# Weights that begin at four different byte offsets, by the step's number, in a one-core FFT and feed-forward kernel

## The chip, the cores and the metric

The kernel runs on one core of one Trainium2 chip. The metric is the device time of one execution in microseconds (us). TensorE (PE in the profile) multiplies, VectorE (DVE) and ScalarE (ACT) round, add and copy, GpSimd (POOL) folds inputs, SyncE (SP) issues most transfers. A matmul has two operands in the on-chip memory SBUF: the weights (stationary, 128x128), which a separate instruction LDWEIGHTS loads (PEld in the profile), and the moving operand, which is streamed past them. Its sum goes to PSUM.

## The reference

x is 8 x 3136 x 256. The real part of its two-dimensional Fourier transform over the last two axes is x'. Each row of x' (256 values) is normalized, goes through two matrices with a ReLU between them, and is added back:

```python
X = np.fft.fft(np.fft.fft(x, axis=1), axis=2)
x = X.real.astype(np.float32)
xn = (x - mean(x)) / sqrt(var(x) + 1e-06) * g_ln      # over the last axis
ch = np.maximum(xn @ w_ch1, 0.0) @ w_ch2              # 256 -> 1024 -> 256
return x + ch
```

## The kernel before

The first two thirds of the transform are small matmuls with tables of sines and cosines (lines 255 to 313: steps 1 and 2 of a mixed-radix transform, `step1`, `step2`). The last axis' transform is folded into the first matrix: `w1` is multiplied by a table in the prologue (`transform_w1`), so that the main loop multiplies the half-transformed rows (`ck`, "chunks" of 256 columns) straight by it. The residual x' itself comes from two short matmuls per tile with the table `ty_s` (`residual`, line 428).

The main loop runs over steps s. A chunk c has 8 steps, one for each 128 of the 1024 hidden values (f = s mod 8), and there are 49 chunks, so 392 steps. In a step

- `moe1_a(s)` multiplies the chunk by 128 columns of the first matrix: two halves j of three matmuls each (line 354), with weights `w1_hi` or `w1_lo` and moving operand `ckh` or `ckl` (`ck_hi`, `ck_lo`);
- ACT and DVE form h from the two halves (lines 359 to 361), `moe1_b(s - 1)` rounds the step before with ReLU into `h_hi` and what is left into `h_lo` (lines 368 and 369);
- `moe2(s - 3)` multiplies h of three steps back by the second matrix: four products of three matmuls each (line 404), with weights `h_hi` or `h_lo` and moving operand `w2_hi` or `w2_lo`.

Each product is three matmuls because the values are split into a rounded part (hi) and a rest (lo), both in the type fp32r; hi x hi, hi x lo and lo x hi are summed in PSUM. So a step has 6 + 12 = 18 matmuls of 256 columns, each with a weight load of its own. Between some steps stand the short matmuls of `step2` (line 309), `residual` (line 428), `step1` (line 262, three of 512 columns) and `step1_ends`.

The order on PE, ACT, DVE and POOL is the order in which the program is written (the tables `after` and `late` say behind which step a piece stands); a tile pool hands out buffers in turn by tag.

Two pools matter here. `moving` holds the moving operands, `weights` the weights. A tile `margin` makes the pool `moving` begin at a multiple of 256 bytes, and a tile `offset` of 64 bytes shifts everything in `weights`: `w1_hi`, `w1_lo`, the four buffers each of `h_hi` and `h_lo`, `t1_hi`, `t1_lo` and `s2` all begin 64 bytes past a multiple of 256. A slice of 128 columns is 512 bytes, so the weights of every matmul of lines 354 and 404 begin 64 bytes past a multiple of 256, and their moving operands at a multiple of 256.

`tw_all` (the table by which w1 is transformed) and `warm_h` (zeros for the matmuls that warm up TensorE) have memory of their own in the pool `const`.

Of the kernel before, what the change touches and what calls it, by code (L numbers as in the profile page):

```python
# [20 lines left out]
F32 = mybir.dt.float32  # L21
F32R = mybir.dt.float32r
# [6 lines left out]
NB, N, D, FF = 8, 3136, 256, 1024  # L29
# [7 lines left out]
MAXW = LASTR + 2 * NB  # L37
CKW = 320
HW = 576
NS = 14  # L40
ROWS = NB * N
NU = NS // 2
KP = 8 * NS

# [17 lines left out]
def tables():  # L62
# [15 lines left out]
    vs = ((0, np.arange(1, 15)), (1, np.append(np.arange(15, NV), 0)))  # L78
    tab = np.zeros((2, 2, 2, NS, 2, HALF))
    tz = np.zeros((4, NS, 50))  # L80
    t = 0
# [17 lines left out]
    tab = tab.transpose(3, 0, 1, 2, 4, 5).reshape(112, 2, HALF)  # L99
    tz = np.concatenate([tz.reshape(4 * NS, 50), np.zeros((KP - 4 * NS, 50))])  # L100
    d = np.arange(1, 129)[:, None]
# [17 lines left out]
def input_rows():  # L119
# [3 lines left out]

    v = np.full((2, NS), -1)
    v[0] = np.arange(1, 15)
# [21 lines left out]
def tile_kernel(ctx: ExitStack, tc: tile.TileContext, x, g_ln, w1, w2, tu, tab, tz, ty, tw, out):  # L147
    nc = tc.nc
    moving = ctx.enter_context(tc.tile_pool(name="moving", bufs=1))
    weights = ctx.enter_context(tc.tile_pool(name="weights", bufs=1))  # L150
    const = ctx.enter_context(tc.tile_pool(name="const", bufs=1))
    work = ctx.enter_context(tc.tile_pool(name="work", bufs=2))
# [3 lines left out]
    moving.tile([128, 32], F32, name="margin")  # L156
    w2_hi = moving.tile([128, 8, D], F32R, name="w2_hi")
    w2_lo = moving.tile([128, 8, D], F32R, name="w2_lo")
    weights.tile([128, 16], F32, name="offset")
    w1_hi = weights.tile([128, 2, FF], F32R, name="w1_hi")  # L160
    w1_lo = weights.tile([128, 2, FF], F32R, name="w1_lo")
    t1_hi = weights.tile([128, 128], F32R, name="t1_hi")
    t1_lo = weights.tile([128, 128], F32R, name="t1_lo")
    tu_s = const.tile([128, 388], F32, name="tu_s")
    tab_s = const.tile([KP, 2, HALF], F32, name="tab_s")
    tz_s = const.tile([KP, 50], F32, name="tz_s")
    tw_all = const.tile([128, 640], F32, name="tw_all")
    tw_s = tw_all[:, :512].rearrange("p (i j k) -> p i j k", i=2, j=2)
    minus = const.tile([128, 128], F32R, name="minus")
    ty_s = const.tile([128, 2, 130], F32, name="ty_s")  # L170
# [27 lines left out]
    def fold_zw(b, i, eng):  # L198

        if i > 3 and b == 0:  # L200
            t = weights.tile([128, HW], F32, tag="h_hi", name=f"zw{b}_{i}", bufs=4)
        else:
# [79 lines left out]
    def width(c):  # L282
        return MAXW if c == LC else CW

    def first_token(m):
        b, j = divmod(m, 8)
        return b * REG + max(gb[2 * j] - 2, 0)
# [52 lines left out]
    def moe1_a(s, passes=((0, 1), (1, 0), (0, 0))):  # L340
        c, f = divmod(s, 8)
        w = width(c)
        ch = chunk[c][1:]
        fs = slice(128 * f, 128 * f + 128)
        wt = (w1_hi, w1_lo)
        if w <= CW:
            ab = psum.tile([128, 2, CW], F32, tag="ab", name=f"ab{s}", bufs=2)
            pa, pb = ab[:, 0], ab[:, 1]
        else:
            pa = psum.tile([128, MAXW], F32, tag="ab", name=f"aa{s}", bufs=2)  # L350
            pb = psum.tile([128, MAXW], F32, tag="fft", name=f"bb{s}")
        for j, pt in ((0, pa), (1, pb)):
            for n, (wi, xi) in enumerate(passes):
                nc.tensor.matmul(pt, wt[wi][:, j, fs], ch[xi][:, j, :w],  # L354
                                 start=(n == 0), stop=(n == 2))
        asb = work.tile([128, MAXW], F32, tag="asb", name=f"asb{s}")
        h = hh[s] = work.tile([128, 2 * CW], F32, tag="h", name=f"h{s}", bufs=4)
        m = 2 * CW - w
        nc.scalar.copy(asb[:, :w], pa)  # L359
        nc.vector.tensor_tensor(out=h[:, :w], in0=asb[:, :w], in1=pb, op=ALU.add)  # L360
        nc.vector.tensor_tensor(out=h[:, w:], in0=asb[:, :m], in1=pb[:, :m], op=ALU.subtract)  # L361

    def moe1_b(s):
        h = hh[s]
        n = 2 * CW
        h_hi = weights.tile([128, HW], F32R, tag="h_hi", name=f"h_hi{s}", bufs=4)[:, :n]
        h_lo = weights.tile([128, n], F32R, tag="h_lo", name=f"h_lo{s}", bufs=4)
        nc.scalar.activation(h_hi, h, AF.Relu)  # L368
        nc.vector.scalar_tensor_tensor(out=h_lo, in0=h, scalar=0.0, in1=h_hi.bitcast(F32),  # L369
                                       op0=ALU.max, op1=ALU.subtract)  # L370
        hh[s] = (h_hi, h_lo)
# [195 lines left out]
    psw = {}  # L567
# [6 lines left out]
                             stop=(i == 1))  # L574

    def w1_cols(t, k, j):
        return t[:, j, 512 * k:512 * k + 512]

    def round_w1(k):
        for j in range(2):  # L580
            nc.scalar.copy(w1_cols(w1_hi, k, j), psw[k, j])

    def rest_w1(k):

        for j in range(2):
            nc.tensor.matmul(psw[k, j], minus, w1_cols(w1_hi, k, j), start=False, stop=True,
                             skip_group_check=True)

    def rest_w1_copy(k):
        for j in range(2):  # L590
            nc.scalar.copy(w1_cols(w1_lo, k, j), psw.pop((k, j)))

    def finish_w2(n):
        _, e, f = conv.pop(f"w2_{n}")
        nc.vector.scalar_tensor_tensor(out=f, in0=f, scalar=2.0 ** -20, in1=e, op0=ALU.mult,
                                       op1=ALU.mult)
        return f
# [19 lines left out]
    for m in range(3, 64):  # L617
        s = 8 * (first_token(m) // CW) - 3
# [26 lines left out]
    for c in range(LC):  # L645
        s = 8 * c + (5 if c > 1 else 6)
# [14 lines left out]
        add_late(8 * LC + y, residual_y, LC, i)  # L661

    warm = work.tile([128, 2 * D], F32, tag="fold", name="warm")
    warm_h = const.tile([128, 2 * D], mybir.dt.bfloat16, name="warm_h")

    def warm_up(n, zeros):

# [5 lines left out]
    with tc.manual_schedule(engines={E.PE, E.Activation, E.DVE, E.Pool}):  # L673
        with tc.manual_schedule(engines={E.SP}):
# [71 lines left out]
            transform_w1(0, 0)  # L746
            transform_w1(0, 1)
            round_w1(0)
            convert_m("w1_3", w1p[3])
            convert_b("w1_3")  # L750
# [8 lines left out]
            convert_z("w2_0", w2p[0])  # L759
            convert_z("w2_1", w2p[1])  # L760
            rest_w1_copy(0)
            transform_w1(1, 1)
            round_w1(1)
            convert_m("w2_0", w2p[0])
            convert_b("w2_0")
            f = finish_w2(0)
# [7 lines left out]
            step2(1, "hl", 0)  # L774
            f = finish_w2(1)
            moe1_a(0, ((1, 0), (0, 0), (0, 1)))
            split_w2(1, f)
            step2(0, "f")
            moe1_a(1, ((1, 0), (0, 0), (0, 1)))
            rest_w1(1)  # L780
            moe1_b(0)
            moe1_a(2)
            moe1_b(1)
            moe1_b(2)
            moe1_a(3)
            rest_w1_copy(1)
            step2(1, "f")
            convert_a("w2_2", w2p[2])
# [5 lines left out]
            f = finish_w2(2)  # L794
# [51 lines left out]
```

## Time and profile before

| what | before |
|---|---|
| device time, median of 3 runs | 1007.62 us (1007.08 to 1007.76) |
| the profiled execution | 1007.27 us, its span 1005.5 us |
| PE busy | 995.1 us, 99% of the span, 8289 matmuls |
| DVE, ACT, POOL busy | 812.3 us (81%), 540.1 us (54%), 243.9 us (24%) |
| granted TensorE clock | 1.000 |

The span runs from the first to the last instruction. A matmul's duration in the profile (276 to 286 ns for 256 columns) is longer than the distance from one start to the next, since matmuls overlap; where matmuls follow each other without a wait, it is the distance between starts that adds up to the span.

### The profile page before, as it was taken

What the parts mean: (1) busy time and instruction counts of PE and PEld (TensorE: products, weight loads), DVE (VectorE), ACT (ScalarE), POOL (GpSimd) and SP (SyncE); (2) the same over time, 40 slices, a digit from 0 to 9 for tenths busy, and PEclk for the clock granted to TensorE, in tenths of its full rate; (3) what the DMA queues carried; (4) which work ended last, traced back from release to release, by engine and by line L of the source; (5) the groups of instructions that cost most, each with busy time, mean ns of one, the idle gap of its engine ahead of it and who ended that gap; (6) DMA issues with size and microseconds to landing.
All of it is one profiled execution on the core that took longest, in us unless ns stands there. A gap on an engine that the chain in (4) does not pass through costs nothing.

```text
span 1005.5 us, 21770 instructions
## 1 busy us (share of the span) xinstructions
PE 995.1 (99%) x8289; PEld 973.7 (97%) x8289; DVE 812.3 (81%) x2190; ACT 540.1 (54%) x1416; POOL 243.9 (24%) x278
## 2 busy tenths in 40 slices
PE   9999999999999999999999999999999999999998
PEld 6799999999999999999999999999999999999998
DVE  7788887878787788878877887878788788887887
ACT  3655556554555555655456555555555554555553
POOL 2146414530153203440054401532034300000000
PEclk9999999999999999999999999999999999999999
DMA  9933243223122511333132232224101230100101
GB/s 346 266 141 126 85 143 110 86 84 108 62 95 85 157 44 53 103 120 105 44 111 101 74 106 75 84 96 126 55 32 44 74 105 23 43 22 22 43 22 43
DMA packets 41528, 92.10 MB, mean 92 GB/s; under 512 B 4176, under 2 KB 18704, under 8 KB 40528
## 3 DMA queue, kind: packets, MB, share of 16 engines
q1 hardware_dynamic: 40016, 88.87, 27.1%
q8 instruction: 66, 1.08, 0.5%
q0 software_dynamic: 320, 1.05, 0.3%
q10 hardware_dynamic: 1088, 0.79, 0.2%
q14 instruction: 38, 0.31, 0.1%
HBM read 50.32 MB, written 40.37 MB: 90 GB/s over the span
## 4 chain that ended last, share of the span: by engine, by line
PE 88%; DVE 7%; ACT 2%; DMA 2%; issue 1%; SPq 0%; ACTq 0%; DVEq 0%
PE acc L404 49%; PE ab L354 25%; PE ps L309 5%; PE psy L428 4%; PE ps L262 3%; DVE h_lo L369 2%; DVE h L360 1%; DVE h L361 1%; ACT h_hi L368 1%; PE ps L255 1%; PE ps L257 1%; DMA scratch<-s 1%; DMA s<-scratch 1%; DMA xs<-x 0%; DVE st L450 0%
## 5 line engine op out<-in xcount | busy, mean ns | idle before, releaser
L404 PE MATMUL acc<-w_hi,h_lo 128*128 128x256 f32 x1568 | 437.1, 279 | 0.2 <-DVE h_lo L369 0.2
L404 PE MATMUL acc<-w_hi,h_hi 128*128 128x256 f32 x1568 | 436.9, 279 | 0.0
L404 PE MATMUL acc<-w_lo,h_hi 128*128 128x256 f32 x1568 | 436.9, 279 | 0.0
L369 DVE SCALAR_TENSOR_TENSOR h_lo<-h,h_hi 128x512 fp32r<-128x512 f32 x392 | 285.9, 729 | 160.8 <-ACT h_hi L368 159.0
L368 ACT ACTIVATE h_hi<-h 128x512 fp32r<-128x512 f32 x392 | 250.1, 638 | 266.0 <-DVE h L361 265.5
L404 PEld LDWEIGHTS acc<-w_hi,h_hi 128*128 128x128 f32 x1568 | 296.7, 189 | 0.0
L404 PEld LDWEIGHTS acc<-w_lo,h_hi 128*128 128x128 f32 x1568 | 295.3, 188 | 0.0
L404 PEld LDWEIGHTS acc<-w_hi,h_lo 128*128 128x128 f32 x1568 | 294.6, 188 | 0.6 <-DVE h_lo L369 0.4
L354 PE MATMUL ab<-ckl,w_hi 128*128 128x256 f32 x768 | 219.9, 286 | 2.6 <-DVE h L361 2.5
L354 PE MATMUL ab<-ckh,w_lo 128*128 128x256 f32 x768 | 214.5, 279 | 0.5 <-ACT ckh L330 0.3
L354 PE MATMUL ab<-ckh,w_hi 128*128 128x256 f32 x768 | 214.1, 279 | 0.0
L225 POOL TENSOR_TENSOR fl<-f,fh 128x512 fp32r<-128x512 f32 x49 | 64.2, 1309 | 495.5 <-ACT fh L219 489.3
L360 DVE TENSOR_TENSOR h<-asb,ab 128x256 f32<-128x256 f32 x384 | 158.7, 413 | 1.5 <-ACT asb L359 1.5
L361 DVE TENSOR_TENSOR h<-asb,ab 128x256 f32<-128x256 f32 x384 | 158.8, 414 | 0.0
L354 PEld LDWEIGHTS ab<-ckl,w_hi 128*128 128x128 f32 x768 | 144.3, 188 | 6.5 <-issue 2.1
L359 ACT COPY asb<-ab 128x256 f32<-128x256 f32 x384 | 139.0, 362 | 17.6 <-PE ab L354 13.9
L354 PEld LDWEIGHTS ab<-ckh,w_lo 128*128 128x128 f32 x768 | 144.7, 188 | 3.1 <-ACT ckh L330 0.5
L354 PEld LDWEIGHTS ab<-ckh,w_hi 128*128 128x128 f32 x768 | 145.3, 189 | 0.0
L330 ACT CAST ckh<-ps 128x392 fp32r<-128x392 f32 (+49 forms) x112 | 39.8, 356 | 62.3 <-PE ps L309 62.1
L265 ACT COPY s<-ps 128x508 f32<-128x508 f32 x56 | 32.8, 585 | 71.9 <-PE ps L262 58.7
L309 PE MATMUL ps<-tab_s,s 112*128 112x98 f32 (+1 forms) x512 | 65.6, 273 | 0.6 <-DMA s<-scratch 0.6
L309 PEld LDWEIGHTS ps<-tab_s,s 112*128 112x128 f32 x512 | 61.9, 191 | 1.1 <-PE pw L670 1.1
(108 smaller groups left out, 964.8 us busy)
## 6 DMA issues: line engine op xcount, KB each, us to landing
xs<-x SPq DMA_DIRECT2D x56, 512.0 KB, 4.4
out<-o SPq DMA_DIRECT2D x96, 256.0 KB, 3.0
scratch<-s SPq DMA_DIRECT2D x49, 256.0 KB, 2.2
s<-scratch SPq DMA_DIRECT2D x7, 1792.0 KB, 9.7
w1p_all<-w SPq DMA_DIRECT2D x8, 512.0 KB, 8.7
scratch<-s POOLq DMA_DIRECT2D x4, 256.0 KB, 6.3
s<-scratch SPq DMA_DIRECT2D x2, 448.0 KB, 5.8
s<-scratch SPq DMA_DIRECT2D x1, 896.0 KB, 12.2
```

What stands on the lines that cost most here:

```text
L225: nc.gpsimd.tensor_tensor(out=lo, in0=f, in1=hi.bitcast(F32), op=ALU.subtract)
L265: nc.scalar.copy(s[:, :, :, :127], ps[:, :, :, :127])
L309: nc.tensor.matmul(ps[:, h, k0 - base:k1 - base], s2[b][:KP, g, 128 * h:128 * h + 128], tab_s[:, h, k0:k1], start=(h == 0 and g == 2 * j), ...
L330: nc.scalar.copy(hi, src)
L354: nc.tensor.matmul(pt, wt[wi][:, j, fs], ch[xi][:, j, :w], start=(n == 0), stop=(n == 2))
L359: nc.scalar.copy(asb[:, :w], pa)
L360: nc.vector.tensor_tensor(out=h[:, :w], in0=asb[:, :w], in1=pb, op=ALU.add)
L361: nc.vector.tensor_tensor(out=h[:, w:], in0=asb[:, :m], in1=pb[:, :m], op=ALU.subtract)
L368: nc.scalar.activation(h_hi, h, AF.Relu)
L369: nc.vector.scalar_tensor_tensor(out=h_lo, in0=h, scalar=0.0, in1=h_hi.bitcast(F32), op0=ALU.max, op1=ALU.subtract)
L404: nc.tensor.matmul(acc[c, i][:, side], hs[xi][:, h0:h0 + 128], ws[wi][:, f], start=(f == 0 and side == 0 and n == 0), stop=(f == 7 and n = ...
L428: nc.tensor.matmul(ps[:, j, :129 + j], ck[:, j], ty_s[:, j, :129 + j], start=(j == 0), stop=True, skip_group_check=True)
```

## The change

The weights of a step's 18 matmuls begin 72, 112, 152 or 192 bytes past a multiple of 256. `place(f)` counts in elements of 4 bytes: 18 + 10 (f mod 4). In w1 each 128 columns are moved apart by 10 elements within a block of four (`4 * 144` elements for four slices, which lie between elements 18 and 560); the tile grows from 8192 to 9216 bytes a partition. `h_hi` and `h_lo` of step s begin at `place(s + 3)`, so when `moe2` uses them three steps later, its weights have the same offset as those of `moe1_a` beside it: all 18 matmuls of a step share one offset, and the offset changes from step to step. The moving operands stay at multiples of 256.

To make room, the tile `offset` is gone (so `t1_hi`, `t1_lo`, `s2` and the others of the pool begin at a multiple of 256), `h_lo` takes 2304 bytes a buffer in place of 2048, `tw_all` takes one of the three buffers of `ck_lo`, and `warm_h` one of the two of `asb`. The copies that write w1 in the prologue write four runs of 128 in place of one of 512.

```diff
+FIRST, MORE = 18, 10
+
+def place(f):
+    return FIRST + MORE * (f % 4)
...
-    weights.tile([128, 16], F32, name="offset")
-    w1_hi = weights.tile([128, 2, FF], F32R, name="w1_hi")
-    w1_lo = weights.tile([128, 2, FF], F32R, name="w1_lo")
+    w1_hi = weights.tile([128, 2, 2, 4 * 144], F32R, name="w1_hi")
+    w1_lo = weights.tile([128, 2, 2, 4 * 144], F32R, name="w1_lo")
...
-    tw_all = const.tile([128, 640], F32, name="tw_all")
+    tw_all = moving.tile([128, 2 * CKW], F32, tag="ck_lo", name="tw_all", bufs=3)
...
     def moe1_a(s):
-        fs = slice(128 * f, 128 * f + 128)
+        fs = slice(place(f) + 128 * (f % 4), place(f) + 128 * (f % 4) + 128)
...
-                nc.tensor.matmul(pt, wt[wi][:, j, fs], ch[xi][:, j, :w],
+                nc.tensor.matmul(pt, wt[wi][:, j, f // 4, fs], ch[xi][:, j, :w],
...
     def moe1_b(s):
-        h_hi = weights.tile([128, HW], F32R, tag="h_hi", name=f"h_hi{s}", bufs=4)[:, :n]
-        h_lo = weights.tile([128, n], F32R, tag="h_lo", name=f"h_lo{s}", bufs=4)
+        o = place(s + 3)
+        h_hi = weights.tile([128, HW], F32R, tag="h_hi", name=f"h_hi{s}", bufs=4)[:, o:o + n]
+        h_lo = weights.tile([128, HW], F32R, tag="h_lo", name=f"h_lo{s}", bufs=4)[:, o:o + n]
...
     def w1_cols(t, k, j):
-        return t[:, j, 512 * k:512 * k + 512]
+        step = 128 + MORE
+        return t[:, j, k, FIRST:FIRST + 4 * step].rearrange("p (f c) -> p f c", c=step)[:, :, :128]
...
-    warm_h = const.tile([128, 2 * D], mybir.dt.bfloat16, name="warm_h")
+    warm_h = work.tile([128, 2 * D], mybir.dt.bfloat16, tag="asb", name="warm_h")
```

The order of the instructions on every engine stays as it was; only their addresses and buffers differ, but for a wait. On PE, where the first residual follows the first products of the second matrix (`acc`, `psy` and `ck` are PSUM sums and the chunk's buffer; the names behind the arrow are the operands), stood before:

```order
L404 MATMUL acc_1_445<-w_hi,h_hi_452 128x256
L428 MATMUL psy_0_566<-ty_s,ck_344 128x129 [waits DMAHW3_49]
L428 MATMUL psy_0_566<-ty_s,ck_344 128x130
L428 MATMUL psy_1_569<-ty_s,ck_344 128x129
L428 MATMUL psy_1_569<-ty_s,ck_344 128x130
L354 MATMUL ab_576<-ckl_346,w_hi 128x256 [waits DVE_49,Activation_49]
```

and now:

```order
L409 MATMUL acc_1_444<-w_hi,h_hi_451 128x256
L433 MATMUL psy_0_565<-ty_s,ck_343 128x129 [waits DMAHW3_49,PE_49]
L433 MATMUL psy_0_565<-ty_s,ck_343 128x130
L433 MATMUL psy_1_568<-ty_s,ck_343 128x129 [waits PE_49]
L433 MATMUL psy_1_568<-ty_s,ck_343 128x130
L358 MATMUL ab_575<-ckl_345,w_hi 128x256 [waits DVE_49,Activation_49]
```

Nothing moved; two matmuls of this one residual also wait for PE's own earlier work.

More of the change, by code (lines that the diff above doesn't have):

```diff
@@ L576, in w1_cols @@
     def w1_cols(t, k, j):
-        return t[:, j, 512 * k:512 * k + 512]
+        step = 128 + MORE
+        return t[:, j, k, FIRST:FIRST + 4 * step].rearrange("p (f c) -> p f c", c=step)[:, :, :128]
     def round_w1(k):
         for j in range(2):
-            nc.scalar.copy(w1_cols(w1_hi, k, j), psw[k, j])
+            nc.scalar.copy(w1_cols(w1_hi, k, j), psw[k, j].rearrange("p (f c) -> p f c", c=128))
     def rest_w1(k):
@@ L590, in rest_w1_copy @@
         for j in range(2):
-            nc.scalar.copy(w1_cols(w1_lo, k, j), psw.pop((k, j)))
+            nc.scalar.copy(w1_cols(w1_lo, k, j), psw.pop((k, j)).rearrange("p (f c) -> p f c", c=128))
     def finish_w2(n):
```

## The prediction

> **What bounds the kernel now.** I read the page's busy times, slices and chain first.
>
> ```profile
> PE 995.1 (99%) x8289; PEld 973.7 (97%) x8289; DVE 812.3 (81%) x2190; ACT 540.1 (54%) x1416; POOL 243.9 (24%) x278
> PEclk9999999999999999999999999999999999999999
> PE 88%; DVE 7%; ACT 2%; DMA 2%; issue 1%; SPq 0%; ACTq 0%; DVEq 0%
> ```
>
> PE is busy all the time at its full granted clock, and 88% of the chain that ended last is PE. So the time is, nearly, the sum of the distances between matmul starts. Then the groups, shapes kept apart:
>
> ```profile
> L404 PE MATMUL acc<-w_hi,h_lo 128*128 128x256 f32 x1568 | 437.1, 279 | 0.2 <-DVE h_lo L369 0.2
> L404 PE MATMUL acc<-w_hi,h_hi 128*128 128x256 f32 x1568 | 436.9, 279 | 0.0
> L404 PE MATMUL acc<-w_lo,h_hi 128*128 128x256 f32 x1568 | 436.9, 279 | 0.0
> L354 PE MATMUL ab<-ckl,w_hi 128*128 128x256 f32 x768 | 219.9, 286 | 2.6 <-DVE h L361 2.5
> L354 PE MATMUL ab<-ckh,w_hi 128*128 128x256 f32 x768 | 214.1, 279 | 0.0
> ```
>
> The matmuls that the change re-addresses are 3 x 1568 = 4704 of line 404 and 3 x 768 = 2304 of line 354 (with 48 of 264 columns left aside): 7008, and they wait for almost nothing (idle 0.2 to 2.6 us). Only their own pace can give time. Is that pace uniform? I asked for eight windows of 15 us that hold nothing but these matmuls, four and four, PE alone:
>
> ```profile
> 352.00:367.00 15.00, 15.00 (x130) 1.00 0.02 8
> 471.00:486.00 15.00, 15.00 (x130) 1.00 0.06 21
> 706.00:721.00 15.00, 15.00 (x130) 1.00 0.10 35
> 936.00:951.00 15.00, 15.00 (x130) 1.00 0.01 2
> ...
> 372.00:387.00 15.00, 15.00 (x135) 1.00 0.05 19
> 490.00:505.00 15.00, 15.00 (x134) 1.00 0.05 19
> 726.00:741.00 15.00, 15.00 (x135) 1.00 0.05 19
> 862.00:877.00 15.00, 15.00 (x134) 1.00 0.02 8
> ```
>
> The number in brackets counts matmuls that touch the window. It is not: 130 in each of four windows, 134 or 135 in the other four, at the same clock 1.00, with no order in the DMA share. The durations of single matmuls say the same (line 404; least, median and largest duration, then the first and the last start):
>
> ```profile
> L404 PE MATMUL acc<-w_hi,h_lo x23: 281/281/281, 236.4 to 247.7; 128*128 128x256 f32 x23
> ...
> L404 PE MATMUL acc<-w_hi,h_lo x25: 276/276/276, 255.7 to 268.0; 128*128 128x256 f32 x25
> ```
>
> Every one of a stretch takes 281 ns, or every one takes 276. I call these the slow and the fast rhythm. A window of 15 us with matmuls of about 0.28 us holds 15.28 us / spacing of them: 15.28 / 130 = 117.5 ns, 15.28 / 134.5 = 113.6 ns. The counts put the rhythms 3.9 ns apart, the durations 5; I take 4.5 ns.
>
> What ends a rhythm? Around the three matmuls of line 262 at 187 us:
>
> ```profile
> L404 PE MATMUL acc<-w_hi,h_lo x11: 276/276/276, 181.5 to 186.3; 128*128 128x256 f32 x11
> ...
> 186.98 0.39 PE L262 MATMUL ps<-fl,t_hi 128*128 128x512 f32 x1
> 187.21 0.40 PE L262 MATMUL ps<-fh,t_lo 128*128 128x512 f32 x1
> 187.45 0.39 PE L262 MATMUL ps<-fh,t_hi 128*128 128x512 f32 x1
> ...
> L404 PE MATMUL acc<-w_hi,h_lo x8: 281/281/281, 188.4 to 191.6; 128*128 128x256 f32 x8
> ```
>
> The same kind of matmul, with the same kind of operands at the same offsets, is fast before and slow after. So the rhythm is neither a matter of a buffer nor of ACT's or DVE's traffic: it is a state that a break sets and that then holds until the next break. The weight loads show a trace of it, in slow and in fast stretches of 6 us:
>
> ```profile
> L404 PEld LDWEIGHTS acc<-w_hi,h_hi x11: 192/192/192, 240.8 to 245.7; 128*128 128x128 f32 x11
> ...
> L404 PEld LDWEIGHTS acc<-w_hi,h_hi x12: 187/188/188, 257.9 to 263.7; 128*128 128x128 f32 x12
> ```
>
> In the slow rhythm every third load takes 192 ns, in the fast one none does. Loads run beside the stream of the matmul before, so I read the rhythm as how the two fall on each other in time.
>
> How much of the kernel is slow? 437.1 + 436.9 + 436.9 = 1310.9 us over 4704 is 278.7 ns; (278.7 - 276) / (281 - 276) = 54%. The slow rhythm costs 0.54 x 7008 x 4.5 ns = 17.0 us in all.
>
> **The change part by part.** Sums stand against the profiled execution, 1007.27 us (span 1005.5 and 1.8 around it), 0.35 under the median of 1007.62.
>
> *Offsets by step.* No matmul is added or made longer; what changes is where a load reads relative to the stream beside it, and that it jumps by 40 bytes (or back by 120) every 18 matmuls. The trace has no such jump. Bounds: every matmul fast, 17.0 us gained, 990.3 us; every matmul slow, 0.46 x 7008 x 4.5 = 14.5 us lost, 1021.8 us. Between them: a slow stretch now lasts until a break in the program's order, up to eight steps; with the change each step begins with a jump, which I take for a break. The entry behind a break is seen at 252 us:
>
> ```profile
> L354 PE MATMUL ab<-ckl,w_hi x2: 277/322/367, 252.2 to 252.7; 128*128 128x256 f32 x2
> L354 PE MATMUL ab<-ckh,w_lo x2: 276/280/283, 252.4 to 252.8; 128*128 128x256 f32 x2
> L354 PE MATMUL ab<-ckh,w_hi x2: 276/278/279, 252.6 to 252.9; 128*128 128x256 f32 x2
> ```
>
> In order of start the six took 367 (it follows short matmuls), 283, 279, 277, 276, 276: the fast rhythm is reached by a slide over three or four matmuls, so from many starting points, while the slow one shows no pull of this kind. I take four of 18 matmuls at the slow price in every step, 22%, and the rest fast: (0.54 - 0.22) x 7008 x 4.5 = 10.1 us gained. That is my choice between the bounds; a three-matmul slide of 7 + 3 + 1 = 11 ns in each of 392 steps, 4.3 us, would leave 12.7 gained.
>
> *t1, s2, ck and tu_s at a multiple of 256 instead of 64 past it.*
>
> ```profile
> L262 PE MATMUL ps<-fh,t_lo 128*128 128x512 f32 x49 | 19.4, 396 | 0.0
> L262 PE MATMUL ps<-fl,t_hi 128*128 128x512 f32 x49 | 19.2, 393 | 1.1 <-DVE ckl L334 1.1
> L428 PE MATMUL psy<-ty_s,ck 128*128 128x129 f32 x198 | 39.5, 281 | 0.1
> L428 PE MATMUL psy<-ty_s,ck 128*128 128x130 f32 x198 | 38.4, 274 | 0.0
> ```
>
> 147 of line 262 differ by 3 ns among themselves (0.4 us), 396 of line 428 by 7 (2.8 us): I take 0, bounds -3 to +3 us.
>
> *Writes of h_hi and h_lo to other offsets.* ACT and DVE have room there:
>
> ```profile
> L369 DVE SCALAR_TENSOR_TENSOR h_lo<-h,h_hi 128x512 fp32r<-128x512 f32 x392 | 285.9, 729 | 160.8 <-ACT h_hi L368 159.0
> L368 ACT ACTIVATE h_hi<-h 128x512 fp32r<-128x512 f32 x392 | 250.1, 638 | 266.0 <-DVE h L361 265.5
> ```
>
> They stand idle 160.8 and 266.0 us before these instructions, 0.41 us each for DVE; a write slower by less than that is hidden, and what would surface first is line 404 waiting for h_lo, now 0.2 us. Zero.
>
> *Prologue.* `tw_all` is read until 28.7 us plus one duration, and its buffer comes up only for a third chunk, long after the first two are written at 35.0 us; `warm_h` is read at 32.1 us for the last time, before `asb` is first written at 36.7:
>
> ```profile
> L573 PE MATMUL psw<-gw,tw_all x16: 590/592/697, 21.7 to 28.7; 128*128 128x512 f32 x16
> L670 PE MATMUL pw<-warm_h x20: 376/379/379, 6.4 to 32.1; 128*128 128x512 bf16 x20
> L359 ACT COPY asb<-ab x3: 372/372/396, 36.7 to 39.1; 128x256 f32<-128x256 f32 x3
> ```
>
> No wait. The two matmuls of line 428 that now wait for PE itself hold up at most a matmul's end, 0.28 us each, with the next six products queued behind them: 0 to 0.6 us, taken as 0. The eight copies of w1 write as many elements as before: 0.
>
> Sum: 1007.27 - 10.1 = 997.2 us; I forecast 997, with its own range 990 to 1002.
>
> **Rivals.** *No change.* The jump is no break at all, and the rhythm hangs only on the program's own breaks. For it: these alone are seen to set it. Then 54% is drawn anew, since t1's offset and the short matmuls are moved too: a share of 45 to 65% is -2.8 to +3.5 us, 1004 to 1011 us. The Trainium skill would have it so: "SBUF — State Buffer", section "Who interferes with whom", gives PE two independent read ports, one for the moving operand and one for LDWEIGHTS, and says that PE never waits on anyone; by it offsets between the two can't matter and the time stays 1007. The trace agrees in that PE's rhythm ignores the other engines, but two rhythms with one clock, one shape and one kind of operand speak against the rule.
>
> *Slower by the slow rhythm.* The jump is a break that throws the fast rhythm out as well, as line 262 did at 187 us, and 40 bytes on, the slide has no time or does not exist. The point from which it decides is the slow share of 54%: above it the change loses. Three quarters slow is 1007.3 + 0.21 x 7008 x 4.5 = 1013.9, all slow 1021.8.
>
> *Slower by crooked starts.* 72 and 152 are odd multiples of 8 bytes, 64 was a multiple of 64. If each load of such a step takes the 192 ns that slow loads show instead of 188, and the next matmul waits for it, half of 7008 pay 4 ns: 14 us, less whatever of it falls into already slow matmuls, so 1014 to 1021 us. Against it: no weights of the trace begin so. The Trainium skill has a rule on that side: "SBUF — State Buffer", section "Door 1: The DMA port swizzle", says that SBUF is read in lines of 16 bytes and that each crossing to a new line has a price; a start in the middle of a line makes 33 lines of 32. No row here tests it.
>
> *Both rhythms end.* Neither is the floor: the two 14-column matmuls of a group of line 238 span 0.37 us at 0.261 each, so they are 0.11 us apart with hardly anything to stream:
>
> ```profile
> 511.26 0.37 PE L238 MATMUL pse<-e0c,tu_s 128*128 128x14 f32 x2
> ...
> L238 PE MATMUL pse<-e0c,tu_s 128*128 128x14 f32 x14 | 2.6, 261 | 0.0
> ```
>
> Spacing 110 in place of the mean 115.9 (113.5 + 0.54 x 4.5) would be 7008 x 5.9 = 41 us: 966 at the very end; half way, 986.
>
> **How the numbers follow.** Chances: forecast 0.48, both rhythms end 0.08, no change 0.17, slow rhythm 0.17, crooked starts 0.10. A measurement of this kernel can tell about 0.2% (2 us) from no change. Faster by more: 0.47 + 0.08 and a third of no change, 0.60; within it: 0.09, slower: 0.31. The likeliest case gives 997. The range: up from all fast with something of the floor, 986, to 1018, which takes in no change and most of the slow cases; left out are about half of the floor case (0.04) and half of the two slow ones (0.13). Since it holds both signs, the likeliest one's own range is the 990 to 1002 above.
>
> **What would show it.** Right: in a stretch that now is slow throughout, each step shows 276 ns but for its first few matmuls, the mean of line 404 falls from 278.7 to about 277, and loads of 192 ns become rare. No change: whole stretches of 276 and of 281 again. Slow rhythm: 281 nearly everywhere. Crooked starts: steps alternate, slow where f is even. Waits of line 404 for h_lo well above 0.2 us, or DVE's idle time gone, would mean that the writes matter after all. I am wrong if the jump does not reset the rhythm, or resets it to slow.

## The result and the profile after

The changed kernel took 1024.29 us (median of 4 runs, 1023.66 to 1026.75), the kernel before 1007.35 us beside it (4 runs, 1006.25 to 1007.76): a ratio of 1.0174 with a 95% interval of 1.0155 to 1.0194. It is slower by 1.7%; 997 us had been forecast, in a range of 986 to 1018.

The profiled execution of the changed kernel is the longest of the four, 1026.75 us with a span of 1025.0. Its busy times, clock and chain of waits:

```profile
PE 1013.2 (99%) x8289; PEld 991.9 (97%) x8289; DVE 813.8 (79%) x2190; ACT 540.6 (53%) x1416; POOL 244.2 (24%) x278
PEclk9999999999999999999999999999999999999999
PE 89%; DVE 6%; ACT 2%; DMA 1%; issue 1%; ACTq 0%; SPq 0%; DVEq 0%
```

The same 8289 matmuls at nearly the same clock (a mean of 0.998, before 1.000), PE as busy as before and still the chain. So no new wait took more than a small part of the time: PE itself became slower. Its groups, and the instruction that writes h_lo (busy us, mean ns of one | idle before it):

```profile
L409 PE MATMUL acc<-w_hi,h_lo 128*128 128x256 f32 x1568 | 440.1, 281 | 0.1
L409 PE MATMUL acc<-w_hi,h_hi 128*128 128x256 f32 x1568 | 440.2, 281 | 0.0
L409 PE MATMUL acc<-w_lo,h_hi 128*128 128x256 f32 x1568 | 439.9, 281 | 0.0
L358 PE MATMUL ab<-ckh,w_lo 128*128 128x256 f32 x768 | 216.2, 282 | 0.8 <-ACT w_lo L597 0.5
L374 DVE SCALAR_TENSOR_TENSOR h_lo<-h,h_hi 128x512 fp32r<-128x512 f32 x392 | 287.8, 734 | 176.0 <-ACT h_hi L373 174.2
```

The mean of the second product went from 279 to 281 ns, with no idle time ahead of it (0.1 us), and DVE has more slack than before (176.0 us against 160.8). But the mean of durations says little here, since matmuls overlap. What adds up is the distance from one start to the next. I took it from the start times of all matmuls of the first and second product in the trace, gaps of 130 ns and more (waits) left out; the distances by offset are those within a step:

| kernel | mean distance, ns | of that, by the step's offset |
|---|---|---|
| before | 115.8 | 64: 113.33 in fast stretches, 117.78 in slow ones |
| after | 118.2 | 72: 118.44; 112: 119.61; 152: 117.15; 192: 117.64 |

7008 x (118.2 - 115.8) = 16.8 us. The spans differ by 19.5; of the rest, about 2 us lie ahead of the main loop of this one execution, where the first matmuls of step 2 waited longer for a transfer than they had before. About 1 us more lies just behind: from 38 to 40 us the granted clock was 0.50, and the first matmuls of line 358 stood 213 ns apart. The wait, first after, then before (start, duration, matmul, wait and its cause in brackets):

```profile
34.98 0.66 PE L313 MATMUL ps<-tab_s,s 112*128 112x99 f32 x4 [2.24 <-DMA s<-scratch]
```

```profile
33.07 0.66 PE L309 MATMUL ps<-tab_s,s 112*128 112x99 f32 x4 [0.59 <-DMA s<-scratch]
```

Four steps in a row of the changed kernel, with offsets 152, 192, 72 and 112 (least, median and largest duration of one kind of matmul in a window of about 1.7 us per step):

```profile
L409 PE MATMUL acc<-w_hi,h_lo x3: 281/281/281, 879.6 to 880.3; 128*128 128x256 f32 x3
L409 PE MATMUL acc<-w_hi,h_lo x4: 280/280/280, 881.7 to 882.8; 128*128 128x256 f32 x4
L409 PE MATMUL acc<-w_hi,h_lo x4: 277/279/283, 883.8 to 884.9; 128*128 128x256 f32 x4
L409 PE MATMUL acc<-w_hi,h_lo x3: 280/281/284, 886.0 to 886.7; 128*128 128x256 f32 x3
```

In none of these four does the fast rhythm of 276 ns settle, not at a step's end either. In the whole execution it does so in three of the 98 steps at 192 alone, early on (steps 11, 27 and 35 of the 392, counted from 0); in step 27:

```profile
L409 PE MATMUL acc<-w_hi,h_lo x4: 276/276/276, 107.8 to 108.8; 128*128 128x256 f32 x4
```

Over eight steps without a break, 32 matmuls of this kind stand 135 distances apart from the first to the last start (seven steps of 18, and nine):

```profile
L409 PE MATMUL acc<-w_hi,h_lo x32: 274/280/284, 859.7 to 875.6; 128*128 128x256 f32 x32
```

(875.6 - 859.7) / 135 = 117.8 ns by these rounded times (118.1 by the exact ones). This reading, last start less first start over 135, is used below for every kernel.

### The profile page after: what moved, and what is told of

Same layout as the page of the kernel before. It is cut to its first block, busy times and chain, and to the rows that moved or that the text cites. A ratio compares the mean times of both kernels' runs of the same rounds, so it can differ in the third digit from the quotient of the medians.

```text
span 1025.0 us, 21771 instructions
## 1 busy us (share of the span) xinstructions
PE 1013.2 (99%) x8289; PEld 991.9 (97%) x8289; DVE 813.8 (79%) x2190; ACT 540.6 (53%) x1416; POOL 244.2 (24%) x278
## 4 chain that ended last, share of the span: by engine, by line
PE 89%; DVE 6%; ACT 2%; DMA 1%; issue 1%; ACTq 0%; SPq 0%; DVEq 0%
PE acc L409 49%; PE ab L358 25%; PE ps L313 5%; PE psy L433 4%; PE ps L266 3%; DVE h_lo L374 2%; DVE h L364 1%; DVE h L365 1%; ACT h_hi L373 1%; DMA scratch<-s 1%; PE pw L676 1%; PE ps L259 1%; PE ps L261 1%; DMA s<-scratch 0%; DVE st L455 0%
## 5 line engine op out<-in xcount | busy, mean ns | idle before, releaser
L374 DVE SCALAR_TENSOR_TENSOR h_lo<-h,h_hi 128x512 fp32r<-128x512 f32 x392 | 287.8, 734 | 176.0 <-ACT h_hi L373 174.2
L358 PE MATMUL ab<-ckh,w_hi 128*128 128x256 f32 x768 | 216.4, 282 | 0.0
```

The costliest lines, as they stand in the source:

```text
L358: nc.tensor.matmul(pt, wt[wi][:, j, f // 4, fs], ch[xi][:, j, :w], start=(n == 0), stop=(n == 2))
```

## Experiments

Theory at the outset: the offset of the weights sets the pace by itself. Rivals: the jump from step to step costs; the crooked starts 72 and 152 cost; something else in the new layout costs. Five times lie 0.2 to 1.7 us above the range of the theory that they bear out (72, 112, the jumps of 64, both operands moved by 8, and 48). All times are of one run unless a range is given; the kernels that were run several times spread by 0.5 to 3.1 us. The kernel before, run beside them, took 1006.96 to 1008.94.

### One offset for all steps, in the changed layout

```diff
-FIRST, MORE = 18, 10
+FIRST, MORE = 16, 0      # 64 bytes; 18: 72; 28: 112; 38: 152; 48: 192
```

Everything else of the change stays (t1, ty_s and the others 64 bytes earlier, shared slots, w1 in blocks); only the jump goes, and the offset is chosen.

> All weights of lines 358 and 409 begin 64 bytes past a multiple of 256 in every step, in the changed kernel's layout (h_lo of 2304 bytes, table and zeros in shared slots, t1 at 0). If the offsets of the weights alone made the change slower, this is the kernel before in all that counts: 1007 us (1002 to 1011, as the share of the slow rhythm is drawn anew). If the layout around them (t1, s2, the shared slots, the writes of w1) costs, it stays near 1024.

> 72 bytes in every step, no jump. Offset theory (each offset has a pace of its own, 72 a bad one): the 118.4 ns that the changed kernel shows at 72 hold throughout, (118.4 - 115.8) x 7000 = 18 us above before: 1024 to 1027. Jump theory (any constant offset has both rhythms, the jumps alone throw the fast one out): 1002 to 1011.

> 152 bytes in every step. Offset theory: 117.2 ns as in the changed kernel's steps at 152, 10 us above before: 1015 to 1019. Jump theory: 1002 to 1011. If 72 and 152 come out alike although the changed kernel's steps differ by 1.3 ns, the pace of a step comes from how it is entered.

> 192 bytes in every step, changed layout. In the changed kernel and in the one with jumps of 64 the steps at 192 ran at 117.6 and 117.8 ns, which is the slow rhythm of 64. If the pace depends on the offset modulo 128, and these steps were slow only because they were entered from another offset, this is fast as 64 is: 992 to 997. If 192 has no fast rhythm: 117.7 ns throughout, 1018 to 1023.

> 112 bytes in every step. The offset decides the pace, the jump nothing: 119.6 ns as in the changed kernel's steps at 112, so (119.6 - 113.7) x 7000 = 41 us above the run with 64: 1032 to 1037. If jumps matter, 112 alone is nearer to 72 and 152: 1017 to 1029.

| offset, bytes | time, us | mean distance, ns | steps of that offset in the changed kernel, ns |
|---|---|---|---|
| 64 | 993.62 | 113.69 | - |
| 72 | 1028.51 | 118.37 | 118.44 |
| 112 | 1037.20 | 119.97 | 119.61 |
| 152 | 1017.67 | 117.21 | 117.15 |
| 192 | 1022.09 | 117.78 | 117.64 |

Each offset has its own pace, and keeps it to 0.4 ns whether all steps have it or every fourth. The mean of the four, 118.3, is the changed kernel's 118.2: the jump between these four offsets costs nothing beside the offsets themselves. Their stretches of eight steps, at 72, 112, 192 and 152 in this order:

```profile
L409 PE MATMUL acc<-w_hi,h_lo x32: 279/284/285, 861.2 to 877.2; 128*128 128x256 f32 x32
```

```profile
L409 PE MATMUL acc<-w_hi,h_lo x32: 277/283/289, 868.2 to 884.4; 128*128 128x256 f32 x32
```

```profile
L409 PE MATMUL acc<-w_hi,h_lo x32: 279/279/280, 855.4 to 871.3; 128*128 128x256 f32 x32
```

```profile
L409 PE MATMUL acc<-w_hi,h_lo x32: 281/281/281, 832.8 to 848.7; 128*128 128x256 f32 x32
...
L409 PE MATMUL acc<-w_hi,h_lo x32: 274/280/281, 851.6 to 867.3; 128*128 128x256 f32 x32
```

16.0, 16.2, 15.9 and 15.9 or 15.7 us for the same 135 distances, against 15.3 in the fast rhythm. The offset 152 has two rhythms too, but its better one (15.7) is far from 15.3. The offset 192 has the two of 64: all 19 of its undisturbed stretches of eight steps stand 117.78 ns apart, as the slow rhythm does, but in two of the 392 steps, 12 and 29 counted from 0, it holds the fast one. In step 12:

```profile
L409 PE MATMUL acc<-w_hi,h_lo x4: 276/276/276, 65.5 to 66.6; 128*128 128x256 f32 x4
```

So the expectation for 192 without the fast rhythm is right in the time and not in the reason: 192 has it, and all but never enters it.

The surprise is the offset 64: with the weights of all 18 matmuls again 64 bytes past a multiple of 256, the changed layout is faster than the kernel before by 14 us. So the change has two parts that go against each other. I timed this kernel with more runs:

> The kernel with 64 in every step again, timed in five rounds: 992 to 996 us, faster than before by 1.2 to 1.6%.

994.16 us (4 runs, 994.03 to 994.5), before 1007.48 (7 runs): a ratio of 0.9869, interval 0.9852 to 0.9885. It is faster than both kernels. Its groups, and eight steps:

```profile
L409 PE MATMUL acc<-w_hi,h_lo 128*128 128x256 f32 x1568 | 433.4, 276 | 0.2 <-DVE h_lo L374 0.2
L409 PE MATMUL acc<-w_hi,h_hi 128*128 128x256 f32 x1568 | 433.3, 276 | 0.0
L409 PE MATMUL acc<-w_lo,h_hi 128*128 128x256 f32 x1568 | 433.2, 276 | 0.0
...
L409 PE MATMUL acc<-w_hi,h_lo x32: 276/276/276, 851.1 to 866.4; 128*128 128x256 f32 x32
```

A mean of 276 over all 1568 says that the fast rhythm (15.3 / 135 = 113.3 ns) now holds nearly throughout: the 17 us that the slow rhythm cost are back, but by the layout, not by the offsets.

### A jump between straight offsets

```diff
-FIRST, MORE = 18, 10
+FIRST, MORE = 0, 16      # 0, 64, 128, 192 bytes
```

> Jumps kept, but by 64 bytes: 0, 64, 128, 192 by the step's number. Jump theory: each jump throws out the fast rhythm, nearly all matmuls at 281 ns, 1018 to 1024. Theory of crooked starts (odd multiples of 8 are what costs, jumps of whole 64s are harmless): 1002 to 1011. If the prediction's idea of a jump that breaks the slow rhythm were right for straight starts: 990 to 1000.

1024.18 us, as slow as the change itself, with every offset a multiple of 64. By offset: 0 at 119.55 ns, 64 at 116.63, 128 at 118.82, 192 at 117.80. So crooked starts aren't needed to lose. Here one thing does depend on the jump: steps at 64 ran at 116.63 and not at 113.7. I sorted the 98 of them by what they follow and by their last nine distances. Of the 28 that follow short matmuls, 26 end in the fast rhythm; of the 70 that are entered by the jump from 0, 67 end in the slow one. One of each, the jump first:

```profile
L409 PE MATMUL acc<-w_hi,h_lo x4: 281/281/281, 312.6 to 313.7; 128*128 128x256 f32 x4
```

```profile
L409 PE MATMUL acc<-w_hi,h_lo x4: 276/276/276, 323.6 to 324.7; 128*128 128x256 f32 x4
```

So where an offset has both rhythms a jump is a break, but one that leads into the slow rhythm, against the prediction.

### What in the layout brings the fast rhythm

In the kernel before, the rhythm changed at the short matmuls between steps. The change moved several of their operands 64 bytes back: the weights of line 266, t1 (64 to 0 bytes past a multiple of 256), while its moving operand stayed; and both operands of line 433 (the weights ck and the moving operand ty_s, 96 to 32) and of line 313 (s2 and tab_s), so that the distances within these two lines stayed as they were. I put t1 and ty_s back, each alone, in the fast kernel (all weights of the main products at 64), and moved t1 alone in the kernel before:

```diff
 # fast kernel, t1 at 64 (t1_lo alike); in the kernel before, at 0: [:, 48:48 + 128]
-t1_hi = weights.tile([128, 128], F32R, name="t1_hi")
+t1_hi = weights.tile([128, 192], F32R, name="t1_hi")[:, 16:16 + 128]
 # fast kernel, ty_s 64 bytes on
-ty_s = const.tile([128, 2, 130], F32, name="ty_s")
+ty_s = const.tile([128, 2 * 130 + 16], F32, name="ty_s")[:, 16:].rearrange("p (a b) -> p a b", a=2)
```

> As the run with 64 in every step, which came out at 993.6 us, but with t1_hi and t1_lo (weights of line 266, the matmuls of 512 columns between the steps) again 64 bytes past a multiple of 256. Theory t1: t1's offset decides which rhythm these three matmuls hand on; with 64 they flip it as before, the slow rhythm is back to about half, 1004 to 1010. Rival, the short matmuls of lines 313 and 433 (s2, ck and ty_s at other offsets): t1 does nothing, 992 to 996.

1006.54 us, mean distance 115.29. Nearly the whole gain is gone. Around line 266, the fast kernel and then this one:

```profile
L409 PE MATMUL acc<-w_hi,h_lo x11: 276/276/276, 180.1 to 184.9; 128*128 128x256 f32 x11
...
185.55 0.40 PE L266 MATMUL ps<-fl,t_hi 128*128 128x512 f32 x1
...
L409 PE MATMUL acc<-w_hi,h_lo x8: 276/276/276, 186.9 to 190.0; 128*128 128x256 f32 x8
```

```profile
L409 PE MATMUL acc<-w_hi,h_lo x11: 276/276/276, 176.5 to 181.2; 128*128 128x256 f32 x11
...
181.56 0.39 PE L266 MATMUL ps<-fl,t_hi 128*128 128x512 f32 x1
...
L409 PE MATMUL acc<-w_hi,h_lo x11: 281/281/281, 183.3 to 188.3; 128*128 128x256 f32 x11
```

With t1 at 0 the fast rhythm outlives these matmuls; with t1 at 64 they turn it into the slow one, as in the kernel before. They also do the reverse. Sorted by the last eight distances before the three matmuls and the ninth to sixteenth behind them, all 49 places give:

| kernel | t1 | fast stays fast | fast to slow | slow to fast | slow stays slow |
|---|---|---|---|---|---|
| before | 64 | 1 | 21 | 26 | 1 |
| 64 in every step, timed | 0 | 38 | 2 | 9 | 0 |
| the same with t1 at 64 | 64 | 0 | 21 | 20 | 8 |
| before with t1 moved | 0 | 29 | 1 | 19 | 0 |

So with t1 at 64 they mostly swap the two rhythms, which goes with the share of about half in the kernel before; with t1 at 0 they lead into the fast one from either.

> The kernel before, in its own layout, with only t1_hi and t1_lo moved to a multiple of 256. Theory t1: the flip at line 262 is gone, 992 to 998. Rival (the short matmuls, the shared slots): 1004 to 1010.

1004.03 us, 115.10 ns: only 3.7 us of 13. Line 262 no longer throws the fast rhythm out (the first of its places below, and at the second it turns the slow one into the fast), but behind step 2 and the residual, lines 309 and 428, the products are slow:

```profile
167.27 0.40 PE L262 MATMUL ps<-fl,t_hi 128*128 128x512 f32 x1
L404 PE MATMUL acc<-w_hi,h_lo x7: 276/276/276, 169.0 to 171.7; 128*128 128x256 f32 x7
...
172.91 1.08 PE L428 MATMUL psy<-ty_s,ck 128*128 128x129 f32 x8
L404 PE MATMUL acc<-w_hi,h_lo x11: 281/281/282, 174.9 to 179.8; 128*128 128x256 f32 x11
...
180.19 0.39 PE L262 MATMUL ps<-fl,t_hi 128*128 128x512 f32 x1
L404 PE MATMUL acc<-w_hi,h_lo x11: 276/276/277, 181.9 to 186.7; 128*128 128x256 f32 x11
```

> The run with 64 in every step (993.6 us), with ty_s, the moving operand of line 433, put back to 96 bytes past a multiple of 256 from 32. Open is why line 428 led into the slow rhythm in the kernel before with t1 moved (1004.0 us), and line 433 into the fast one in the run with 64. If it is ty_s beside the weights of line 358, the stretches behind line 433 turn slow again: 1000 to 1006. If it is s2 or something else: 992 to 996.

1001.72 us, 114.60 ns: 7.6 us lost by 64 bytes of ty_s (whose weights, `ck`, stay where they are, so this distance is one that neither kernel had). The flip stands behind step 2 and the residual:

```profile
L409 PE MATMUL acc<-w_hi,h_lo x32: 276/276/276, 819.3 to 834.6; 128*128 128x256 f32 x32
...
834.99 1.03 PE L313 MATMUL ps<-tab_s,s 112*128 112x98 f32 x8
835.86 1.08 PE L433 MATMUL psy<-ty_s,ck 128*128 128x129 f32 x8
...
L409 PE MATMUL acc<-w_hi,h_lo x32: 281/281/281, 837.5 to 853.4; 128*128 128x256 f32 x32
```

The time lies in the range expected of ty_s, but ty_s alone is not the entry. Where these two kinds alone stand between the steps, 28 of 29 fast stretches turn slow in the kernel before with t1 moved, and none of 38 in the timed kernel; with ty_s put back it is 10 of 36.

So the addresses of the short matmuls' own operands take part in which rhythm the next stretch of long ones falls into. The layout's gain needs t1 and the entry behind the residual together. Which of the other operands there (ck, s2 and tab_s were moved too) makes up the rest of that entry was not tried.

### Offset or distance, and crooked starts alone

Weights and moving operand (w2, ck_hi, ck_lo) both moved by m elements, so that their distance stays 64 bytes:

```diff
+FIRST, MORE = 32, 0      # m = 16: weights at 128, moving at 64
+FIRST, MORE = 18, 0      # m = 2: weights at 72, moving at 8
+w2_hi = moving.tile([128, 8 * D + 64], F32R, name="w2_hi")[:, m:m + 8 * D].rearrange("p (f d) -> p f d", f=8)
...
-chunk[c] = tuple(p[:, :, :MAXW] for p in parts)
+chunk[c] = tuple(p[:, :, o:o + MAXW] for p, o in zip(parts, (0, m, m)))
```

> Weights at 128 in every step, and the moving operands of lines 358 and 409 (w2, ck_hi, ck_lo) at 64 past a multiple of 256. If what counts is the distance from moving operand to weights, this is 64 again: 992 to 1010, with the fast rhythm at 113.3 ns seen. If what counts is the weights' own address, 128 has the 118.8 ns of the steps at 128 in the run with jumps of 64: 1024 to 1030.

1003.88 us, 115.20 ns, both rhythms of the kernel before, which 128 bytes had not shown in the kernel that jumps by 64:

```profile
L409 PE MATMUL acc<-w_hi,h_lo x32: 276/276/276, 839.7 to 855.0; 128*128 128x256 f32 x32
...
L409 PE MATMUL acc<-w_hi,h_lo x32: 281/281/281, 859.0 to 874.9; 128*128 128x256 f32 x32
```

15.3 and 15.9 us: between these two it is the distance between weights and moving operand that counts, not the offset of the weights by itself.

> Weights at 72 in every step, moving operands of lines 358 and 409 at 8: the distance is 64 again, but both begin at an odd multiple of 8 bytes. If only the distance counts, the fast rhythm (113.3 ns, 276 ns long) is there, and the time lies between 992 and 1010. If a start in the middle of 16 bytes costs by itself, no matmul is at 113.3 ns and the time is 1015 to 1035.

1035.92 us, 120.01 ns, and uniform:

```profile
L409 PE MATMUL acc<-w_hi,h_lo x32: 282/283/283, 867.0 to 883.2; 128*128 128x256 f32 x32
```

16.2 / 135 = 120.0 ns at the distance of 64: operands that both begin 8 bytes past a multiple of 16 cost 6.7 ns a matmul here against the fast rhythm, and the distance alone doesn't settle the pace. So a crooked start does cost, though it doesn't explain the change: 112 is a multiple of 16 and was the slowest of its four offsets.

### Other straight offsets

`FIRST, MORE` of 8, 0 (32 bytes), 12, 0 (48), 20, 0 (80) and 24, 0 (96), to see whether 64 is one good value of many.

> 32 bytes in every step, a multiple of 32 on the other side of 64. Range around 64 of 32 bytes to each side: 992 to 1010. Otherwise 1016 to 1037.

> 48 bytes in every step. If the fast rhythm belongs to a range of distances around 64, it is seen here: 992 to 1010. If 64 alone has it: spacing 117 to 120 ns, 1016 to 1037.

> 80 bytes in every step, 8 from the 72 that has no fast rhythm, and a multiple of 16. Range around 64: 992 to 1010. 64 alone, or starts at multiples of 64 alone: 1016 to 1037.

> 96 bytes in every step, a multiple of 32. Range around 64 of 32 bytes to each side: 992 to 1010. Otherwise 1016 to 1037, as 112.

| offset | 32 | 48 | 80 | 96 |
|---|---|---|---|---|
| time, us | 1025.21 | 1038.72 | 1027.96 | 1021.80 |
| mean distance, ns | 118.30 | 123.3 in 16 of 19 stretches of eight steps, 117.78 in 3 | 118.75 | 117.82 |

None has the fast rhythm. At 48 bytes every second distance is about 130 ns, so there the stretches are read and not the mean with its limit of 130. Eight steps:

```profile
L409 PE MATMUL acc<-w_hi,h_lo x32: 280/286/292, 868.9 to 885.5; 128*128 128x256 f32 x32
```

16.6 / 135 = 123.0 ns. Among the distances 0, 32, 48, 64, 72, 80, 96, 112, 128, 152 and 192 (0 and 128 only in the kernel that jumps by 64), 64 alone holds 113.3 over whole stretches; 192 reaches it in a few single steps.

## Why the prediction was wrong

The sum was 1007.3 - 10.1 (offsets) + 0 (layout). Measured, from 1007.48: -13.3 for the layout (994.16), +30.1 for the offsets (1024.29). Both terms failed, in opposite directions. The distances account for the second: with 1752 matmuls at each offset, against 113.68 in the timed kernel at 64 throughout, 72 costs 8.3 us, 112 10.4, 152 6.1 and 192 6.9, 31.7 in all, near the 30.1 measured.

*The step that failed first: "Offsets by step".* It named the right quantity, where a load falls relative to the stream beside it, and then let the new offset itself cost nothing and took only the jump for an event. The term of -10.1 us came from "each step begins with a jump, which I take for a break", with only four of 18 matmuls slow behind it. The runs show +30.1 us in its place: 72, 112 and 152 bytes have paces of their own (118.4, 120.0 and 117.2 ns with no jump at all) and no rhythm of 113.3 to slide into, and at 192 95 of 98 steps are slow. Where the jump could choose, at 64 in the kernel with jumps of 64, it led into the slow rhythm in 67 of 70 steps. The slide over 367, 283, 279, 277 and 276 ns was read as a pull to the fast rhythm from anywhere; it had been seen at the distance of 64 alone, on which all long matmuls of the trace stood. Nor did "the slow one shows no pull of this kind" hold there: over all 49 places of line 262, 21 of 22 fast stretches came out slow, where one place had been looked at. That the trace held no other distance was seen; the bounds should then have come from somewhere else than the two rhythms of this one. "Every matmul slow, 1021.8" was no upper end: one offset for all steps gave up to 1038.72.

*"t1, s2, ck and tu_s at a multiple of 256", taken as 0 with bounds of 3 us.* This is the term that was mis-sized: -13.3. I priced the short matmuls' own durations, a few ns each. Their price is what they do to the long ones behind them. The pieces were in the trace: the rhythm is set at a break, and line 262 is such a break; I did not conclude from it that whatever changes line 262's addresses may re-draw 17 us. The no-change rival said so ("drawn anew, since t1's offset and the short matmuls are moved too"), but let the draw go from 45 to 65% slow; in the timed kernel 19 of 392 steps end slow.

*What held.* PE's pace carries the whole time, the rhythm persists between short matmuls (in 94 of the 99 stretches of two steps and more in the kernel before, 92 in the timed one), the writes of h_hi and h_lo are hidden, and nothing waits for the shared slots or for psy (no idle time stands before line 433).

*The rivals.* "Slower by the slow rhythm" comes near in number (1021.8 against 1024.29) and is the mechanism of a part alone: of the four offsets only 192 runs at the slow rhythm's pace, 117.6. Its reading of the jump, a break that throws the fast rhythm out, is what steps at 64 show in the kernel with jumps of 64. "Crooked starts" asked for steps that alternate with f, slow at 72 and 152. They don't: 72 and 112 are slow, 152 is the best of the four. The rule beside it, in the Trainium skill, "SBUF — State Buffer", section "Door 1: The DMA port swizzle", prices each crossing of a 16-byte line. The runs at a distance of 64 agree that a start in mid-line costs (120.0 against 113.3 ns), but the rule doesn't sort the offsets: 48, 80 and 112 are multiples of 16, and slower than 152. The other rule of the Trainium skill, "SBUF — State Buffer", section "Who interferes with whom", by which PE's two read ports are independent and PE never waits on anyone, would have these kernels equal; at granted clocks of 0.998 to 1.000, with the same 8289 matmuls in the same order, they took 994 to 1039 us. Here the measurement decides against it. "Both rhythms end" needs a mean distance of less than 113.3 ns, which no run showed.

*Open.* Why only the distances of 64 and, seldom, 192 have the fast rhythm, and whether 192 could be kept in it by other short matmuls; how a matmul of 512 columns swaps the rhythms with t1 at 64, leads into the fast one with t1 at 0, and keeps either (26 fast and 22 slow of 49) with t1 at 0 and the products' operands at 128 and 64; which operand of step 2 or the residual makes the rest of the entry there.

## What to carry to other kernels

When a group's mean lies between two sharp durations, find out what selects between them before forecasting a change in its neighbourhood: here 64 bytes of a small table, used by 147 matmuls between the steps, decided over most of 13 us in 7008 others. Price an address that no row of the trace shows as unknown in both directions, and test it as a constant before varying it. And split a change that moves other things to make room: its side effect was worth -13.3 us and hid behind its own +30.1, and the layout with 64 bytes kept (994.16 us) beats both kernels.

## What was unexpected of the hardware

The mean distance of fp32r matmuls of 256 columns, each with a weight load, went from 113.3 to 123.3 ns by the byte addresses of the two operands, with the same matmuls in the same order at granted clocks of 0.998 to 1.000. Most of the means that held over eight steps are 113.33, 116.66, 117.33, 117.78, 118.67 and 120.00 ns, which are 17, 17 1/2, 17 3/5, 17 2/3, 17 4/5 and 18 times 6.667 ns. The others lie close to such fractions: 118.30 to 118.37 at 72 and 32 bytes to 17 3/4 (118.33), 123.27 to 123.39 at 48 to 18 1/2 (123.33). Single distances are no such multiples: at 112 bytes five of them repeat, 121, 120, 125, 120 and 114 ns, which make 600 ns or 90 units together, and the slow rhythm consists of 117, 118 and 119. So it looks as if a group of a few matmuls took a whole number of such units; what the unit is, no run shows. The same kernel falls into the same rhythms at nearly the same places each time: the two profiled executions of the fastest one agree in 382 of 392 steps.
